# A scan-and-two-layers kernel: block coupling of the inverse done by matmuls in the chain, decays loaded once, other layouts, larger weight pieces and a new cost table for the order

## Chip, cores and metric

One core of a Trainium2 chip runs the whole program. The metric is device time in microseconds (us): the median of several executions. A profile is one execution more, recorded by the hardware profiler.

## What is computed

A recurrent attention over 768 steps for 4 x 8 heads of width 40 (float32), then two layer pairs with float64 weights on the 3072 tokens that it gives.

```python
for t in range(S):                      # S = 768, state (4, 8, 40, 40)
    y[:, :, t] = einsum('bhd,bhde->bhe', rt, state)
    Sa = einsum('bhde,bhe->bhd', state, at)
    state = state * wt[:, :, None, :] - einsum('bhd,bhe->bhde', Sa, bt) + einsum('bhd,bhe->bhde', vt, kt)
x = y as (3072, 320)
x = max(x @ w1, x @ w2, x @ w3) @ w_out             # d_ff 768
out = ((x @ w_a) * (x @ w_b)) @ w_out2              # d_ff 1536
```

## The kernel before

**The scan in chunks.** The 768 steps are cut into 24 chunks of 32, in 12 pairs. Within a chunk the recurrence is solved in closed form: products of decays (two scans on VectorE, DVE), matmuls of keys with the decayed a and b, and the inverse T of a unit triangular 32 x 32 matrix per head. `prep(p)` prepares pair p without the state, `chain(c)` carries the state through chunk c, `gather(p)` sends the pair's output through DRAM (XD) into the layout that the layers take (xf).

**Preparation.** `prep` loads the decays twice, forwards as wf into Pp and backwards as wr into Rp (line 376), the keys KT and a, b (ZL). Per chunk it scans Pp (line 396), takes the reciprocal of its end, scans Rp (line 400), multiplies keys (404) and ZL (414, POOL or DVE), runs matmuls (429 or 447), masks the result into ZL (435 or 454) and stores the 32 x 32 blocks to DRAM as BD (461). They come back one matrix to a partition as BU (467). `solve(p)` inverts on DVE and POOL: the two 16 x 16 diagonal blocks of each matrix by seven growing steps and two products (TW, TX), each a multiplication (501 on POOL, 502 on DVE) and a reduction (503). Then three more products give TC, the off-diagonal block times an inverse diagonal block; ACT lays out TU for them (535). T goes out as TD (473) and back as TT (477); TC goes out as ED (482) and back into NB (485), whose diagonal blocks are the identity.

**Chain.** In `chain(c)`: Z (620), copy Zs on ScalarE (ACT, 626); half (634) multiplies TT with Zs; copy Zy (638); umm (647) multiplies NB with Zy; copies XX, XU (657, 658); then the new state (held 672, smm 667, copies to ST and ZR) and, beside it, the output: transpose XT (703, 706), G (715), mask into YL (719), Y (733), scaling into XY (737). The values vt load into XT at 565.

**Layers.** `weights_a` cuts the float64 weights of the first layer pair into two float32r halves, in 24 pieces: a load (773), four conversions on DVE (763 to 766), copies (780), and for the first three of six blocks matmuls with the identity (790 to 793), for the others a subtraction and an addition (797, 798). `moe_a(p)` runs the first layer pair on the 256 tokens of pair p (841, 866 to 870) as soon as all its weights and xf are there, and stores X2D. `stage_b` cuts nine of the twelve blocks of the second layer pair's weights in 18 pieces into DRAM (WD, 933 to 941), `weights_b` loads them once the scan is done, `live_b` cuts the other three directly, and `moe_b(n)` runs the second layer pair on 512 tokens (995, 1003 to 1005), six times.

**What sets the order.** Nothing above is the order of issue. Every operation goes to a planner (`Plan`) with an engine, an estimated duration, what it reads and writes, PSUM banks and a priority (smaller first). `run` places one operation after another by these estimates; the result is one fixed order for each engine, and each engine executes it in order. DMAs go out on SyncE's queue (SP) in order, too: a DMA that waits holds up those behind it. `keep` inserts filler matmuls (line 277) where TensorE (PE) would be idle by plan. Eight PSUM banks are shared, with limits by kind (`LIMITS`).

Priorities: chain 0.001c, prep -0.5 + 0.6p, `weights_a` 2.0, `moe_a` 2 + p, `stage_b` 3.0, each less 0.04 times the remaining path.

## Time and profile before

| | us |
|---|---|
| median of 3 runs | 1065.24 (1064.34 to 1067.66) |
| the profiled execution | 1075.56 |
| its span, first to last instruction | 1073.8 |
| PE busy in the span | 1024.6 (95%) |
| DVE busy | 642.5 (60%) |
| ACT busy | 501.1 (47%) |
| POOL busy | 248.9 (23%) |

PE counts as busy while any matmul is in flight, so short waits hide under the end of the matmul before, and fillers count as work. A wait is put down to the event that came last. Start times are from the start of the span.

### The profile page before, as it was taken

Reading aid. Unit: us, or ns where it says so; the run is one execution under the profiler, and the core shown is the slowest. Engines: PE = TensorE matmul, PEld = TensorE weight load, DVE = VectorE, ACT = ScalarE, POOL = GpSimd, SP = SyncE. Lnnn points to the kernel's source line nnn. Section 1 sums busy time; section 2 is a strip of 40 time slices with the busy share of each in tenths; the row PEclk is TensorE's granted clock in tenths of the full one; section 3 lists DMA queues with packets and bytes.
Section 4 is the critical chain, followed back from the end, with each engine's and each line's share of the span. In section 5 each row is a group of like instructions: output and inputs, shape, how many; then the busy total and the mean of one; then the engine's idle time right before and its main releaser. Section 6 shows DMA issues by size and latency. Waiting matters only on the chain.

```text
span 1073.8 us, 34324 instructions
## 1 busy us (share of the span) xinstructions
PE 1024.6 (95%) x14888; PEld 920.8 (86%) x14888; DVE 642.5 (60%) x1046; ACT 501.1 (47%) x1157; POOL 248.9 (23%) x201
## 2 busy tenths in 40 slices
PE   8999888999899889989999999999999999999997
PEld 7877787988898888888899999888888888888886
DVE  7977688796789686979798333474232232332222
ACT  5337657476757566646567422243222232322221
POOL 3423366342336242343433100011000000000000
PEclk9989889899999999999999999999999999999999
DMA  8936966757776866666565448532001000000000
GB/s 271 207 75 147 195 149 140 166 133 187 162 187 143 198 159 146 169 165 169 152 167 136 115 125 246 144 97 74 1 11 45 1 26 1 7 19 1 25 1 28
DMA packets 173437, 123.10 MB, mean 115 GB/s; under 512 B 122464, under 2 KB 147168, under 8 KB 172320
## 3 DMA queue, kind: packets, MB, share of 16 engines
q1 hardware_dynamic: 170688, 116.41, 43.7%
q10 hardware_dynamic: 2592, 4.42, 1.2%
q8 instruction: 119, 1.95, 0.8%
q14 instruction: 38, 0.31, 0.1%
HBM read 93.07 MB, written 27.72 MB: 112 GB/s over the span
## 4 chain that ended last, share of the span: by engine, by line
PE 68%; DVE 11%; DMA 9%; issue 5%; ACT 3%; SPq 3%; POOL 1%; ACTq 0%; POOLq 0%; DVEq 0%
PE bank L995 25%; PE bank L841 11%; PE bank L1003 4%; PE bank L1005 4%; PE bank L1004 4%; PE bank L277 3%; DMA BU<-BD 2%; PE bank L733 2%; PE bank L715 2%; PE bank L647 1%; DMA WD<-wraw 1%; PE bank L866 1%; DVE TP L502 1%; DVE wraw L764 1%; PE bank L620 1%
## 5 line engine op out<-in xcount | busy, mean ns | idle before, releaser
L1013 DVE TENSOR_TENSOR bas<-bank,bas 128x512 f32<-128x512 f32 x72 | 49.7, 691 | 193.0 <-PE bank L995 186.5
L995 PE MATMUL bank<-bxhi,bw 128*128 128x512 f32 x576 | 156.3, 393 | 0.0
L995 PEld LDWEIGHTS bank<-bxhi,bw 128*128 128x128 f32 x576 | 106.0, 188 | 20.6
L1012 ACT ACTIVATE bas<-bank 128x512 f32<-128x512 f32 x72 | 43.0, 598 | 142.8 <-PE bank L995 142.8
L1015 ACT ACTIVATE bgh<-bas 128x512 fp32r<-128x512 f32 x72 | 45.5, 632 | 132.1 <-DVE bas L1013 132.1
L841 PE MATMUL bank<-xhi,whi 128*128 128x256 f32 x432 | 95.4, 303 | 0.0
L995 PE MATMUL bank<-bxlo,bw 128*128 128x512 f32 x288 | 89.7, 393 | 0.0
L841 PE MATMUL bank<-xhi,wlo 128*128 128x256 f32 x432 | 87.6, 284 | 2.1 <-issue 2.1
L841 PE MATMUL bank<-xlo,whi 128*128 128x256 f32 x432 | 87.9, 285 | 1.1 <-DVE xlo L830 1.1
L1003 PE MATMUL bank<-bo,bgh 128*128 128x320 f32 x288 | 88.9, 309 | 0.0
L1005 PE MATMUL bank<-bo,bgl 128*128 128x320 f32 x288 | 88.9, 309 | 0.0
L1004 PE MATMUL bank<-bo,bgh 128*128 128x320 f32 x288 | 88.8, 308 | 0.0
L856 DVE TENSOR_TENSOR hm<-bank,hm 128x512 f32<-128x512 f32 x72 | 49.5, 688 | 50.7 <-PE bank L841 46.7
L1016 DVE TENSOR_TENSOR bgl<-bas,bgh 128x512 fp32r<-128x512 f32 x72 | 50.4, 701 | 42.9 <-ACT bgh L1015 42.6
L414 POOL TENSOR_TENSOR ZL<-ZL,Pp 64x512 f32<-64x512 f32 x39 | 56.4, 1446 | 64.5 <-DVE Pp L396 51.2
L841 PEld LDWEIGHTS bank<-xlo,whi 128*128 128x128 f32 x432 | 67.9, 193 | 3.7 <-issue 2.2
L277 PE MATMUL bank<-con 128*128 128x128 f32 x482 | 67.6, 296 | 2.9 <-DMA con<-in_con_dram 2.9
L841 PEld LDWEIGHTS bank<-xhi,whi 128*128 128x128 f32 x432 | 66.7, 192 | 3.2
L277 PEld LDWEIGHTS bank<-con 128*128 128x128 f32 x482 | 62.7, 208 | 5.9 <-ACT bank L345 2.9
L841 PEld LDWEIGHTS bank<-xhi,wlo 128*128 128x128 f32 x432 | 67.4, 192 | 0.0
L995 PEld LDWEIGHTS bank<-bxlo,bw 128*128 128x128 f32 x288 | 54.1, 188 | 12.3
L841 PE MATMUL bank<-xl,wt 128*128 128x256 f32 x216 | 61.6, 285 | 0.4 <-DVE xl L834 0.4
(182 smaller groups left out, 2447.5 us busy)
## 6 DMA issues: line engine op xcount, KB each, us to landing
wraw<-in_wpb_dram SPq DMA_DIRECT2D x18, 480.0 KB
KT<-in_kb_dram SPq DMA_DIRECT2D x20, 384.0 KB
Pp<-in_wf_dram SPq DMA_DIRECT2D x10, 528.0 KB
Rp<-in_wr_dram SPq DMA_DIRECT2D x10, 528.0 KB
wraw<-in_wpa_dram SPq DMA_DIRECT2D x12, 384.0 KB
bw<-WD SPq DMA_DIRECT2D x9, 512.0 KB
WD<-wraw ACTq DMA_DIRECT2D x18, 240.0 KB
WD<-wca SPq DMA_DIRECT2D x18, 240.0 KB
```

Source lines behind the costliest of these rows:

```text
L277: P.keep = lambda b: T.matmul(bank[b][:, 0:128], ident, ident, start=True, stop=True)
L414: op("POOL", po(512), lambda w_, cc=cc, g=g, r0=r0: G.tensor_tensor(Z_[r0:r0 + 64, cc, g], Z_[r0:r0 + 64, cc, g], P_[r0:r0 + 64, cc, :, 0: ...
L841: T.matmul(ps, w, x, start=(i == 0), stop=(i == 7))
L856: op("DVE", dv(512, True), lambda w_, pn=pn: V.tensor_tensor(f(hm), bank[w_[pn]], f(hm), ALU.max), r=[pn], w=["hm"], fin=[pn], pri=ep)
L995: T.matmul(ps, w, x, start=(k == 0), stop=(k == 7))
L1003: T.matmul(o, gh[:, c], oh, start=ff == 0, stop=False)
L1004: T.matmul(o, gh[:, c], ol, start=False, stop=False)
L1005: T.matmul(o, gl[:, c], oh, start=False, stop=ff == 11)
L1012: op("ACT", ac(512), lambda w_, j=j, pa=pa: A.activation(tb["as", j], bank[w_[pa]], AF.Copy), r=[pa], w=[("bas", j)], fin=[pa], pri=ep)
L1013: op("DVE", dv(512, True), lambda w_, j=j, pb=pb: V.tensor_tensor(tb["as", j], bank[w_[pb]], tb["as", j], ALU.mult), r=[pb], w=[("bas", j) ...
L1015: op("ACT", ac(512), lambda w_, j=j, k=k: A.activation(tb["gh", k], tb["as", j], AF.Copy), r=[("bas", j)], w=[("gh", k)], pri=ep)
L1016: op("DVE", dv(512), lambda w_, j=j, k=k: V.tensor_tensor(tb["gl", k], tb["as", j], tb["gh", k], ALU.subtract), r=[("bas", j), ("gh", k)], ...
```

## The change

**Coupling.** For the first KS = 6 pairs `solve` returns after T: no TC, TU, ED. The off-diagonal block goes from BD straight into NB, whose diagonal blocks are zero. The chain runs half (T Zs), then lift, which adds NB times -T Zs to the bank of Z, a second copy into Zs, then last (T Zs) for the result. The bank of Z is freed after the second copy. From pair 6 on it is as before (with TU stored transposed).

**Decays.** One load Wp, in two halves of 48 partitions (64 in pair 0), feeds both scans; the second reads and writes backwards, into Rr. wr is gone.

**Values.** vt is stored with the head running fastest, so that each row of XT is one run of 2 KB; the copy of line 706 writes, and the weights of line 715 read, at a step of 16 elements.

**Pieces.** `weights_a` takes 12 pieces (768 and 512 columns) in place of 24, `stage_b` 9 pieces of 960 columns in place of 18. The buffers are larger.

**Order.** The planner gets new estimates: DMAs pass one after another at a fixed rate (`line`), POOL and DVE operations of two SBUF inputs exclude each other (`port`, `Both`), operations on PE are planned with a margin after what they wait for (`PMD`, `PME`), and a change of tile form on PE costs. Priorities: `weights_a` 0.3, `stage_b` 8.0, prep -0.5 + 0.45p.

```diff
+KS = 6
 NSPL = 2
 DMIN = 0.4
 NPB = 3
 NH = 2
-WP = 2.0
+WP = 0.3
...
-LAT = {"PE": 0.2, "ACT": 0.15, "DVE": 0.14, "POOL": 0.08}
+LAT = {"PE": 0.25, "ACT": 0.1, "DVE": 0.1, "POOL": 0.12}
+XRATE = 270e3
+XWAY = 1.8
+XISS = 0.46
+XQ = 1.0
+SLOPE = 0.45
+PMD = 0.7
+PME = 0.2
+PRE0 = -0.5
+EPA = 0.6
+GPR = 0.2
+SBP = 8.0
+MAP = 2.0
+MODE = 0.1
...
+                    if o["xfer"]:
+                        s = max(s, line - XQ)
+                    if eng == "POOL" or isinstance(o["ways"][eng][0], Both):
+                        s = max(s, port)
...
+            if eng == "POOL" or isinstance(o["ways"][eng][0], Both):
+                port = e
+            if o["xfer"]:
+                line = max(line, s + 1.0) + o["xfer"]
+                end = line + o["lat"]
...
+                mg = (PMD if o["xfer"] else PME) if "PE" in q else 0.0
+                est[j] = max(est[j], e if len(q) == 1 and eng in q and eng != "DVE" and o["lat"] is None else end + mg)
...
-        return 0.15 + n * 0.00105 if ps else 0.12 + n * 0.0014
+        return 0.15 + n * 0.00105 if ps else Both(0.13 + n * 0.00108)
 
     def ac(n):
-        return 0.17 + n * 0.0009
+        return 0.17 + n * 0.00086
 
     def po(n):
-        return 0.4 + n * 0.0023
+        return 0.2 + n * 0.0021
 
     def dma(fn, nbytes, r=(), w=(), pri=0.0, pre=1.2):
-        return op("SP", max(DMIN, nbytes / 300e3), fn, r=r, w=w, pri=pri, lat=1.4 + nbytes / 250e3, pre=pre)
+        return op("SP", XISS, fn, r=r, w=w, pri=pri, lat=XWAY, pre=pre, xfer=nbytes / XRATE)
...
+    Wp = ap_.tile([128, 2, NU * 33 + 1], F32, name="Wp")
+    Rr = ap_.tile([128, 2, NU * 33 + 1], F32, name="Rr")
+    Rp = [Rr[:, i, 1:NU * 33 + 1].rearrange("p (u s) -> p u s", s=33)[:, :, 1:33] for i in range(2)]
...
-            for t_, n, w in ((P_, "wf", [(k, b, c, g) for c in cs for k in ("P", "Pc") for g in range(2)]), (Rp, "wr", [(k, c, g) for c in cs for k in ("R", "Rc") for g in range(2)])):
-                dma(lambda w_, t_=t_, n=n, c0=c0, c1=c1: SP.dma_start(t_[:, c0:c1].rearrange("p c u s -> p c (u s)"), ia[n][p].rearrange("p (c f) -> p c f", c=2)[:, c0:c1]), 270e3 * (c1 - c0), w=w, pri=pr)
+            for g in range(2):
+                nr, src = (64, ia["wf0"][g]) if not p else (48, ia["wf"][p, g])
+                dma(lambda w_, g=g, nr=nr, src=src, c0=c0, c1=c1: SP.dma_start(Wp[GP[g]:GP[g] + nr, c0:c1], src[:, c0:c1]),
+                    nr * 2116 * (c1 - c0), w=[("W_", c, g) for c in range(c0, c1)], pri=pr)
...
-            op("DVE", 1.4, lambda w_, cc=cc: V.tensor_tensor_scan(
-                P_[:, cc].rearrange("p u s -> p (u s)"), P_[:, cc].rearrange("p u s -> p (u s)"),
+            op("DVE", Both(1.26), lambda w_, cc=cc: V.tensor_tensor_scan(
+                P_[:, cc].rearrange("p u s -> p (u s)"), Wp[:, cc, 0:NU * 33],
                 d1.rearrange("p u s -> p (u s)"), 0.0, ALU.mult, ALU.add), r=kp + ["d1"], w=pc, pri=pr)
-            op("DVE", 0.25, lambda w_, cc=cc: V.reciprocal(d1[:, :, 0:1], P_[:, cc, :, 32:33]), r=pc, w=["d1"], pri=pr)
-            op("DVE", 1.4, lambda w_, cc=cc: V.tensor_tensor_scan(
-                Rp[:, cc].rearrange("p u s -> p (u s)"), Rp[:, cc].rearrange("p u s -> p (u s)"),
+            op("DVE", 0.25, lambda w_, cc=cc: V.reciprocal(d1[:, :, 0:1], P_[:, cc, ::-1, 32:33]), r=pc, w=["d1"], pri=pr)
+            op("DVE", Both(1.26), lambda w_, cc=cc: V.tensor_tensor_scan(
+                Rr[:, cc, NU * 33:0:-1], Wp[:, cc, NU * 33:0:-1],
                 d1.rearrange("p u s -> p (u s)"), 0.0, ALU.mult, ALU.add),
-               r=[("R", cc, 0), ("R", cc, 1), "d1"], w=rc, pri=pr)
+               r=kp + ["d1"], w=rc, pri=pr)
...
+        nb = NB[p % 2]
+        if p in (KS, KS + 1):
+            unit(p % 2, pr)
+        if p < KS:
+            for j in range(4):
+                dma(lambda w_, j=j: SP.dma_start(
+                    nb[32 * j:32 * j + 16].rearrange("p c h t -> p (c h) t")[:, :, 16:32],
+                    BD[b].rearrange("(ch pqx) s t -> pqx s ch t", pqx=4)[j][0:16, :, 16:32]),
+                    16e3, r=bk, w=[("NB", p % 2, j)], pri=pr)
...
+        if p < KS:
+            return
...
-        prod(TC, 0, 16, BU, 16, 32, TU, 0, 16, 8, 8, 8, k, ["TC"])
-        prod(TC, 8, 16, BU, 16, 32, TU, 8, 16, 8, 8, 16, k, ["TC"])
+        prod(TC, 0, 16, BU, 16, 32, TU, 0, 1, 8, 8, 8, k, ["TC"], 16)
+        prod(TC, 8, 16, BU, 16, 32, TU, 128, 1, 8, 8, 16, k, ["TC"], 16)
...
-        dma(lambda w_: SP.dma_start(XT[0:80, :, 0, :], ia["vt"][c].rearrange("p (u t) -> p u t", t=32)),
-            328e3, w=[("XTv", 0), ("XTv", 1)], pri=pr, pre=4.0 if c else 1.2)
+        dma(lambda w_: SP.dma_start(XT[0:80, 0:C * NU], ia["vt"][c]),
+            260e3, w=[("XTv", 0), ("XTv", 1)], pri=pr, pre=4.0 if c else 1.2)
...
-                                     Z_[:, cc, g, bb * 4 + j, :], ZR[z][:, g, bb * 2 + pq, 1 - x, :], start=True, stop=True)
-
-        op("PE", 0.95, zmm, act=0.23,
+                                     Z_[:, cc, g, bb * 4 + j, :], ZR[z][:, g, bb * 2 + pq, 1 - x, :], start=p >= KS or (bb == 0 and g == 0), stop=p >= KS, skip_group_check=p < KS)
...
+        def lift(w_):
+            for k in range(8):
+                for j in range(4):
+                    T.matmul(bank[w_[pz]][32 * j:32 * j + 32, k * 40:k * 40 + 40],
+                             NB[p % 2][32 * j:32 * j + 32, cc, k, :], Zy[32 * j:32 * j + 32, k, :], start=False, stop=True, skip_group_check=True)
+
+        def last(w_):
+            for bb in range(B):
+                for g in range(2):
+                    for j in range(4):
+                        k, n = g * 4 + bb, bb * 2 + g
+                        T.matmul(bank[w_[pu]][32 * j:32 * j + 32, n * 40:n * 40 + 40],
+                                 T_[32 * j:32 * j + 32, cc, k, :], Zs[32 * j:32 * j + 32, k, :], start=True, stop=True)
+
+        if p < KS:
+            op("PE", 0.72, lift, md="32", r=["Zy"] + [("NB", p % 2, j) for j in range(4)], w=[pz], act=0.045, pri=pr)
+            op("ACT", ac(320), lambda w_: A.activation(
+                Zs.rearrange("p k d -> p (k d)"), bank[w_[pz]][:, 0:320], AF.Copy, scale=-1.0), r=[pz], w=["Zs"], fin=[pz], pri=pr)
+            op("PE", 0.72, last, md="32", r=["Zs"] + [("TT", b, j) for j in range(4)], w=[pu], ps=[pu], act=0.045, pri=pr)
+        else:
+            op("PE", 0.72, umm, md="32", r=["Zy"] + [("NB", p % 2, j) for j in range(4)], w=[pu], ps=[pu], act=0.045, pri=pr)
...
-                    T.matmul(ps[64 * x:64 * x + 64, u * 64:u * 64 + 64], XT[0:80, 2 * u + x].rearrange("p k s -> p (k s)"), RB[0:80, :, 2 * u + x], start=True, stop=True)
-
-        op("PE", 1.26, gmm, r=[("XTu", 0), ("XTu", 1), ("XTv", 0), ("XTv", 1), ("RB", 0), ("RB", 1)], w=[pg], ps=[pg], act=0.45, pri=0.2 + pr)
+                    T.matmul(ps[64 * x:64 * x + 64, u * 64:u * 64 + 64], XT[0:80, 2 * u + x::NU], RB[0:80, :, 2 * u + x], start=True, stop=True)
...
+            for q in range(1):
+                pr = SBP
+                cs = slice(0, 960)
+                dma(lambda w_, ff=ff, cs=cs: SP.dma_start(r, ia["wpb"][ff][:, cs].bitcast(U32).rearrange("p (m k) -> p m k", k=2)), 983e3, w=wk + ["sr", "sw"], pri=pr)
+                convert(lambda: r, lambda: a, 960, "sr", "sa", pr, w=ck)
```

## Rows read from the trace of the kernel before

**Rows 1.** Busy time by stage: stage, us; each engine's busy us; granted clock, DMA.
```profile
0.00:150.00 150.00, 137.02 (x2604) 116.83 (x2605) 118.95 (x195) 83.89 (x219) 63.05 (x57) 0.94 0.71 172
150.00:200.00 50.00, 44.23 (x937) 39.65 (x937) 38.75 (x68) 30.94 (x81) 24.67 (x20) 0.83 0.63 152
25.00:250.00 225.00, 207.58 (x4369) 180.50 (x4368) 185.56 (x304) 133.13 (x347) 100.25 (x82) 0.92 0.65 151
200.00:594.00 394.00, 369.51 (x8225) 342.06 (x8225) 318.18 (x525) 249.69 (x612) 149.90 (x113) 0.99 0.67 164
```

**Rows 2.** The same for line 277's fillers alone: PE, PEld, clock, DMA.
```profile
0.00:150.00 150.00, 55.79 (x392) 51.86 (x392) 0.94 0.71 172
```

**Rows 3.** PE's first layer matmul, and ACT's copies of weights with first and last start.
```profile
148.86 0.48 PE L841 MATMUL bank<-xhi,whi 128*128 128x256 f32 x2
...
L780 ACT ACTIVATE wt<-wraw x12: 357/368/391, 22.6 to 194.8; 64x192 fp32r<-64x192 f32 x12
```

**Rows 4.** End of the chain of waits through the scan: start us, us, what.
```profile
628.14 1.35 PE bank L733 x64
...
653.40 9.60 PE bank L841 x80
```

**Rows 5.** PE in order of time, half and umm of chunks 0, 1, 10, 11.
```profile
64.17 1.29 PE L634 MATMUL bank<-Zs,TT 32*32 32x40 f32 x64
74.16 0.79 PE L647 MATMUL bank<-Zy,NB 32*32 32x40 f32 x64
87.78 0.79 PE L634 MATMUL bank<-Zs,TT 32*32 32x40 f32 x64
91.85 1.06 PE L647 MATMUL bank<-Zy,NB 32*32 32x40 f32 x64
298.94 0.79 PE L634 MATMUL bank<-Zs,TT 32*32 32x40 f32 x64
311.73 0.79 PE L647 MATMUL bank<-Zy,NB 32*32 32x40 f32 x64
322.91 0.97 PE L634 MATMUL bank<-Zs,TT 32*32 32x40 f32 x64
327.77 0.79 PE L647 MATMUL bank<-Zy,NB 32*32 32x40 f32 x64
```

**Rows 6.** Chunk 6: Z in the chain of waits, then half on PE.
```profile
190.69 1.23 PE bank L620 x64
...
214.92 0.42 PE L634 MATMUL bank<-Zs,TT 32*32 32x40 f32 x4
```

**Rows 7.** DVE groups of 0 to 250 us: busy us, mean ns | idle before.
```profile
L502 DVE TENSOR_TENSOR TP<-BU,TU 128x512 f32<-128x512 f32 x7 | 8.3, 1185 | 4.7 <-ACT TU L535 4.7
L503 DVE TENSOR_REDUCE TC<-TP 128x32 f32<-128x512 f32 x10 | 6.7, 677 | 0.0
L503 DVE TENSOR_REDUCE TC<-TP 128x64 f32<-128x512 f32 x5 | 3.4, 673 | 0.0
```

**Rows 8.** DVE in order of time, one conversion of 384 and one of 192 columns.
```profile
68.04 0.56 DVE L764 SCALAR_TENSOR_TENSOR wraw<-wraw,wca 128x384 uint32<-128x384 uint32 x1
86.05 0.36 DVE L764 SCALAR_TENSOR_TENSOR wraw<-wraw,wca 128x192 uint32<-128x192 uint32 x1
```

**Rows 9.** Mask of pair 5's blocks on DVE, then SP's queue, in order of time.
```profile
248.56 1.73 DVE L435 TENSOR_TENSOR ZL<-bank,con 64x256 f32<-64x256 f32 x4
...
255.75 2.44 SPq L485 DMA_DIRECT2D NB<-ED  x2
...
259.93 0.97 SPq L461 DMA_DIRECT2D BD<-ZL  x2
```

**Rows 10.** PE's line 715 in the chain of waits; DVE with and without steps.
```profile
622.08 1.08 PE bank L715 x32
...
70.80 1.04 DVE L502 TENSOR_TENSOR TP<-TW,TXp 128x512 f32<-128x512 f32 x1
250.32 0.69 DVE L859 TENSOR_TENSOR hlo<-hm,hhi 128x512 fp32r<-128x512 f32 x1
```

More of the change, by code (lines that the diff above doesn't have):

```diff
@@ L109, in run @@
         done, last, top = 0, 0, 0.0
+        line, port, mode = 0.0, 0.0, None
         busy = {}
@@ L154, in run @@
                         f = s + o["ways"][eng][0] + o["ways"][eng][2]
-                        if any(max(free_t.get(e, 0.0), est[i]) + w[0] + w[2] < f for e, w in o["ways"].items() if e != eng):
+                        if any(max(free_t.get(e, 0.0), est[i], port if e == "POOL" or isinstance(w[0], Both) else 0.0) + w[0] + w[2] < f for e, w in o["ways"].items() if e != eng):
                             continue
@@ L207, in run @@
                     dur *= 2
+                if o["md"] != mode:
+                    dur += MODE if o["md"] else 0.0
+                elif mode:
+                    dur -= MODE
+                mode = o["md"]
                 spend(s, s + dur, o["act"])
@@ L230, in run @@
                 q = self.ops[j]["ways"]
-                est[j] = max(est[j], e if len(q) == 1 and eng in q and eng != "DVE" and o["lat"] is None else end)
+                mg = (PMD if o["xfer"] else PME) if "PE" in q else 0.0
+                est[j] = max(est[j], e if len(q) == 1 and eng in q and eng != "DVE" and o["lat"] is None else end + mg)
                 if not left[j]:
@@ L350, in setup @@
         for i in range(2):
-            op("ACT", ac(512), lambda w_, i=i: A.activation(
-                NB[i].rearrange("p c h t -> p (c h) t"), TC.rearrange("p i j -> p (i j)")[:, 0:32].unsqueeze(1).to_broadcast([128, 16, 32]), AF.Copy), r=["TC"], w=[("NB", i, j) for j in range(4)], pri=-3)
+            zero(NB[i], [("NB", i, j) for j in range(4)], "POOL", pri=-3)
         dma(lambda w_: SP.dma_start(TXp, ia["eye"]), 270e3, w=["TX"], pri=-0.55)
@@ L385, in prep @@
         for cc in range(2):
-            kp = [("P", b, cc, g) for g in range(2)]
+            kp = [("W_", cc, g) for g in range(2)]
             pc = [("Pc", b, cc, g) for g in range(2)]
@@ L409, in prep @@
+            op("POOL", 2.25, kmul(G), r=rc + [("K", kb_, cc, 0), ("K", kb_, cc, 1)], w=kc, pri=pr, alt=[("DVE", dv(1024), kmul(V))])
+            for src, k, n in ((Rp[cc], rc, 1), (P_[:, cc, :, 1:33], pc, 0)):
                 op("ACT", 0.61, lambda w_, cc=cc, src=src, n=n: A.activation(
-                    Rp[:, cc, :, 0:32], src, AF.Square, accum_out=gd[:, 4 * p + 2 * cc + n:4 * p + 2 * cc + n + 1]),
+                    Rp[cc], src, AF.Square, accum_out=gd[:, 4 * p + 2 * cc + n:4 * p + 2 * cc + n + 1]),
@@ L480, in prep @@
                 130e3, r=[("TD", b, h) for h in range(2)], w=[("TT", b, j)], pri=pr)
-        for h in range(2):
+        for h in range(2 if p >= KS else 0):
             dma(lambda w_, h=h: SP.dma_start(ED[b][:, 8 * h:8 * h + 8, :], TC[64 * h:64 * h + 64]), 33e3, r=["TC"], w=[("ED", b, h)], pri=pr)
-        nb = NB[p % 2]
-        for j in range(4):
+        for j in range(4 if p >= KS else 0):
             dma(lambda w_, j=j: SP.dma_start(
@@ L488, in prep, with unit @@
                 16e3, r=[("ED", b, h) for h in range(2)], w=[("NB", p % 2, j)], pri=pr)
+    def unit(i, pr):
+        op("ACT", ac(512), lambda w_: A.activation(
+            NB[i].rearrange("p c h t -> p (c h) t"), con[:, 192:224].unsqueeze(1).to_broadcast([128, 16, 32]), AF.Copy), r=["con"], w=[("NB", i, j) for j in range(4)], pri=pr)
     def solve(p):
-        pr = -0.5 + 0.6 * p
+        pr = PRE0 + SLOPE * p
         cnt = [0]
@@ L635, in half @@
                              T_[32 * j:32 * j + 32, cc, k, :], Zs[32 * j:32 * j + 32, k, :], start=True, stop=True)
-        op("PE", 0.9, half, r=["Zs"] + [("TT", b, j) for j in range(4)], w=[ph], ps=[ph], act=0.045, pri=pr)
-        op("ACT", ac(320), lambda w_: A.activation(Zy.rearrange("p k d -> p (k d)"), bank[w_[ph]][:, 0:320], AF.Copy), r=[ph], w=["Zy"], fin=[ph], pri=pr)
+        op("PE", 0.72, half, md="32", r=["Zs"] + [("TT", b, j) for j in range(4)], w=[ph], ps=[ph], act=0.045, pri=pr)
+        op("ACT", ac(320), lambda w_: A.activation(Zy.rearrange("p k d -> p (k d)"), bank[w_[ph]][:, 0:320], AF.Copy, scale=1.0 if p >= KS else -1.0), r=[ph], w=["Zy"], fin=[ph], pri=pr)
         pu = ("a", "u", c)
@@ L910, in open_w @@
             tb["gl", i] = w.tile([128, 512], F32R, name=f"bgl{i}")
+        for i in range(2):
+            tb["lr", i] = w.tile([128, 1024], F32, name=f"blr{i}")
+            tb["lc", i] = w.tile([128, 512], F32, name=f"blc{i}")
     def open_x():
@@ L1208, in layout @@
     o["aa"] = pair(em(a)).reshape(NP, 2, D, 2, -1)
-    for n in ("wf", "wr"):
-        z = np.ones((NP, 2, 64, 2, NU, 33), f)
-        z[..., 0] = 0
-        z[:, :, 0:D] = o[n].reshape(NP, 2, D, 2, NU, 33)
-        o[n] = z.reshape(NP, 128, -1)
+    z = np.ones((NP, 2, 64, 2, NU * 33 + 1), f)
+    z[..., ::33] = 0
+    z[:, :, 0:D] = pair(wf).reshape(NP, 2, D, 2, NU * 33 + 1)
+    o["wf"], o["wf0"] = np.ascontiguousarray(z[:, :, 0:48]), np.ascontiguousarray(z[0])
     for n, m in (("kb", 2),):
```

171 lines of the change are left out of this document (79 added, 92 removed).

## The prediction

> **What bounds the kernel now.** I read the page first, then the table of stages, then TensorE's lines in order of time, then DVE's and the DMA queue's around one pair. The page has TensorE (PE) busy nearly throughout; the reader is to see that this is not a full PE. By stage, the span of 1073.8 us is 673 us of scan with the first layer pair, and 400 us of the second layer pair, whose matmuls the change leaves alone; I carry these 400 us over. In the first 150 us, 55.8 of the 137.0 busy us are the filler matmuls of line 277 [rows 1, 2]. From 150 to 200 us the granted clock averages 0.83, that is some of the time at 1.2 instead of 2.4 GHz, which loses 0.17 x 50 = 8.5 us, and PE idles 5.8 us [rows 1]; the first layer of pair 0 begins at 148.9 and is held up there, since the last of its weights are cut at 194.8 [rows 3]. From 200 to 594 us PE idles 24.5 us [rows 1]. So most of the loss lies in the first 200 us, and the end is PE's backlog behind the chain: the last chunk's output matmuls start at 628.1 and the backlog runs to 673 without a gap [rows 4].
>
> What feeds PE is the chain of 24 chunks, and that is fed by the preparation of each pair (loads, scans, inverse, round trips over DRAM). From 25 to 250 us DVE is busy 185.6 of 225 us, 82% [rows 1]: this engine sets the pace of the early preparations. A preparation shows twice in the chain: as a wait for the inverse T ahead of the half matmuls (line 634), and as a wait for the coupling block NB ahead of line 647.
>
> **The change part by part.** The sum is made against the profiled execution (span 1073.8, its time 1075.56 us). That stands 10.3 us, 1%, above the median of the three runs, 1065.24; I take the difference in us off the median.
>
> Coupling on PE. In the first six pairs NB no longer needs three products and three reductions on DVE or POOL and the round trip TC, ED, NB; it comes straight from BD. For that each of 12 chunks runs half, lift, last in place of half, umm: one more group of 64 matmuls and one more ACT copy, both inside the dependent chain. Call the time from the start of one group to the start of the next dependent one a step. Half to umm took 9.99, 4.08, 15.18, 4.29, 8.96, 12.79 us in the six first chunks, 55.3 in all, and 4.07, 7.14, 3.91, 1.86, 3.12, 4.86 us in the six second ones, median 4.0; the first and the last of each six are in [rows 5]. First chunks wait for NB, second ones show the bare step. Its bounds are therefore 1.9 and 7.1 us; I take 3.5, near the median. First chunks: 6 x 2 x 3.5 = 42 against 55.3, a gain of 13. Second chunks: 6 x 3.5 = 21 more. Of these I let four of six hide, because the next pair's half waits for T anyway (24 us in chunk 6 [rows 6]): 7 remain. Net -6, with bounds -33 (12 x 1.9 against 55.3, all second ones hidden) and +73 (12 x 7.1 against 55.3, and 6 x 7.1 more). PSUM bank z is now held from Z through the wait for T, out of eight; what that costs is inside the upper bound. PE's own work grows by 12 groups of at most 0.79 us [rows 5], 9 us. Half falls into the first 200 us, where fillers cover it: +4, bounds 0 and +9. Where that cover is gone, it is the 9.
>
> DVE's relief. In the first 250 us the removed products and reductions cost DVE 8.3 + 6.7 + 3.4 = 18.4 us [rows 7]. Of the weight pieces, four conversions for each of 24 pieces become four for each of 12. Two conversions of 192 columns take 2 x 0.36 us against 0.56 for one of 384 [rows 8], 0.16 more; four times that is 0.64 us for a piece saved, times 12 = 7.7 us. Together 26 us, and at DVE's 82% share 21 us of the early preparations: -21, bounds 0 (something else comes last) and -26.
>
> Decays once. The second decay load is gone, and the first keeps 64 or 48 rows of 128. By the shapes the first two pairs load 0.95 MB instead of 2.16, 1.2 MB less, which at the 172 GB/s of the first 150 us [rows 1] is 7 us of transfers; only part of it stands in front of the first inverse: -3, bounds -7 and 0. Both scans now read one buffer (a reload must wait for both scans of the pair before, and what SP has queued behind that load waits too). This costs nothing while a load has most of a pair's time, some 45 us; if that cover goes, it is one load's latency in a pair. Reversed reading covers as many elements; I take the scan's time as unchanged.
>
> SP's queue. ED and NB stand in order with all else. At chunk 8 SP is with NB from 255.75 on, and the BD store of the next pair, ready at 250.3, goes out at 259.9 [rows 9]. With ED gone from six preparations and half as many weight loads such delays are rarer; but the NB loads stay, and loads of 983 KB, twice the old size, now stand in front of small ones. The bytes are the same, hits half as often and twice as long: I take -2, bounds -10 (one such delay) and +10.
>
> Values in long rows. 1280 short runs a chunk become 80 long ones. No long wait of PE for them is in the trace, so 0. The price is elsewhere: the weights of line 715 are now read at a step of 64 bytes. The trace has no strided weight load; these 32 matmuls take 1.08 us at unit step. The nearest strided row is DVE's product of 512 with one operand at a large step, 1.04 us against 0.69 for a unit-step subtraction [rows 10]: a factor 1.5, which here is 24 x 0.54 = 13 us. Bounds 0 and 13; I take 0, since weight loads overlap matmuls. The Trainium skill, "SBUF — State Buffer", section "SBUF: two separate sides", speaks against this edit: SBUF is read in lines of 16 bytes, and accesses that each go to a new line pay a penalty, so that fp32 strides about four elements for free; this one strides sixteen. By that rule the 13 us would belong in the sum, by TensorE's own row nothing.
>
> Order with room. Weight pieces move from priority 2.0 to 0.3, ahead of the preparations of pairs 2 and up; the cutting of the second layer pair's weights moves behind. If the first pieces are cut by about 150 us instead of 195, pair 0's first layer (192 matmuls at the 0.12 us of [rows 4], 23 us) falls into time that holds fillers and idle now. That lets PE's backlog at the end shrink as much as the chain does; without it the chain's gain only lengthens the backlog. I cost it at 0, and T is what comes last again.
>
> Sum: -6 + 4 - 21 - 3 - 2 = -28, so 1065 - 28 = 1037 us.
>
> **The rivals.** (1) More. PE also gets back what the sum leaves lying: half of the 24.5 us idle from 200 to 594 (12), the 8.5 us of clock, the 7 us of second chunks. That is -28 - 27 = -55, 1010 us. For it: 55.8 us of fillers are room enough. Against: T is still waited for. (2) The strided weights cost their 13 us on a full PE: 1050 us; the skill's rule would make it so. (3) No relief. T is set by DMA round trips, not by DVE, so the 21 us fall away, and half the strided price (6) eats the rest: 1064 us. For it: the six first chunks lose 55 us to a round trip. (4) A long step. If ACT and PE place other work between half, lift and last, the step is 5 us, not 3.5, and if T comes early enough that nothing hides, the chain changes by 12 x 5 + 6 x 5 - 55.3 = +35; with the other terms (-22) that is +13, 1078 us. It decides from a step of 77.3/18 = 4.3 us on. For it: one step took 7.14 us, and the median is 4.0. Against: waits for T like that of [rows 6].
>
> **How the numbers follow.** Forecast 0.49 (its own range, about half the way to the bounds of its two largest terms, 1022 to 1054), more 0.20, strided 0.07, no relief 0.08, long step 0.16. Faster by over 0.3%, which is about what a measurement of this kernel can tell from no change: 0.49 + 0.20 + 0.07 = 0.76; within it 0.08; slower 0.16. The range reaches from somewhat below the second case to short of the last, 1004 to 1073, and leaves out a tail of the fast case and most of the slow one.
>
> **What would show it.** Right: the last chunk's output matmuls start near 600 instead of 628; half to lift and lift to last are 3 to 4 us each; 18 reductions into TC instead of 36; the last weights are cut before 160 and pair 0's first layer is done by about 180; fillers in the first 150 us are well below 56; the 32 matmuls of line 715 still take 1.08 us. Wrong: steps above 4.3 us, T as late as now in pairs 2 to 5, or more idle time of PE between 200 us and the end of the chain, which an order made from misjudged durations would show.

## The result and the profile after

| | before | after |
|---|---|---|
| median of 17 runs, us | 1068.24 (1064.34 to 1074.50) | 1075.79 (1073.44 to 1079.86) |
| ratio, 95% interval | | 1.0073 (1.0053 to 1.0092) |
| span of the profiled execution, us | 1073.8 | 1072.2 |
| PE busy, us | 1024.6 | 1039.1 |
| DVE, POOL busy, us | 642.5, 248.9 | 596.8, 133.1 |

The change makes the kernel slower by 0.7%, some 8 us. The forecast was 1037 us, 28 us of gain. The two profiled executions differ by less than the medians, and the other way: that of before (1075.56 us, granted clock 0.980) took longer than any of its 17 runs, and that of after (1073.94 us, clock 0.990) is the second shortest of its 17, whose clocks average 0.985. So the traces tell where the time sits, and the ratios tell how much it is.

Busy time by stage, as in [rows 1]: stage, us, then PE, PEld, DVE, ACT, POOL, granted clock, DMA share, GB/s.

```profile
0.00:150.00 150.00, 142.34 (x3093) 121.22 (x3097) 107.61 (x177) 84.49 (x219) 27.24 (x28) 0.99 0.67 166
150.00:200.00 50.00, 45.85 (x1010) 42.38 (x1001) 38.34 (x54) 29.68 (x72) 14.41 (x14) 0.93 0.46 122
25.00:250.00 225.00, 215.32 (x4969) 187.39 (x4967) 165.01 (x272) 136.70 (x346) 46.29 (x40) 0.98 0.58 144
200.00:594.00 394.00, 378.97 (x8735) 356.03 (x8734) 288.72 (x492) 265.95 (x622) 89.71 (x79) 0.99 0.59 151
```

DVE has its relief: 165.0 of 225 us from 25 to 250 where [rows 1] have 185.6, and POOL falls from 100 to 46. The granted clock of that stretch is 0.98 and was 0.92. PE idles 15.0 us from 200 to 594, down from 24.5. Everything that was to feed PE better does so.

The fillers of the first 150 us (line 313 now, as in [rows 2]), and the start of the first layer with the last cut of a weight (as in [rows 3]):

```profile
0.00:150.00 150.00, 51.56 (x390) 48.34 (x390) 0.99 0.67 166
```

```profile
157.16 0.51 PE L909 MATMUL bank<-xhi,whi 128*128 128x256 f32 x2
```

```profile
L854 ACT ACTIVATE wt<-wraw x12: 359/370/394, 51.4 to 199.2; 64x192 fp32r<-64x192 f32 x12
```

The weights are not cut earlier: 199.2 against 194.8, the first layer starts at 157.2 against 148.9, and the fillers are nearly as many.

The last of the first layer's matmuls, before and after: count, ns, first and last start.

```profile
L841 PE MATMUL bank<-xl,wt x216: 277/283/415, 149.9 to 672.3; 128*128 128x256 f32 x108
L909 PE MATMUL bank<-xl,wt x216: 279/283/415, 158.1 to 670.4; 128*128 128x256 f32 x108
```

The chain of waits at its end, as in [rows 4]: start us, us, what.

```profile
603.91 2.04 PE bank L786 x32
...
609.00 1.35 PE bank L804 x64
...
651.45 9.60 PE bank L909 x80
```

The last chunk's output starts at 609.0, 19 us earlier than the 628.1 of [rows 4]. But the longest run of first-layer matmuls stands at 651.5, where it stood at 653.4: the lead of the chain is gone 40 us later, and the first layer ends at 670.4 where it ended at 672.3. And the G group takes 2.04 us, where [rows 10] have 1.08.

PE around half (685), lift (704) and last (712) in chunks 0 and 10, as in [rows 5]:

```profile
55.27 0.79 PE L685 MATMUL bank<-Zs,TT 32*32 32x40 f32 x64
58.23 0.79 PE L704 MATMUL bank<-Zy,NB 32*32 32x40 f32 x64
60.27 0.79 PE L712 MATMUL bank<-Zs,TT 32*32 32x40 f32 x64
...
289.46 0.79 PE L685 MATMUL bank<-Zs,TT 32*32 32x40 f32 x64
292.01 0.54 PE L704 MATMUL bank<-Zy,NB 32*32 32x40 f32 x34
...
295.51 0.79 PE L712 MATMUL bank<-Zs,TT 32*32 32x40 f32 x64
```

The steps are short: 2.96 and 2.04 us, 2.55 and 3.50 us; over all twelve chunks the 24 steps average 3.23 us.

PE's busy time in the fillers and in G, before and after, then in lift: busy us, mean ns, idle before it.

```profile
L277 PE MATMUL bank<-con 128*128 128x128 f32 x482 | 67.6, 296 | 2.9 <-DMA con<-in_con_dram 2.9
...
L715 PE MATMUL bank<-RB,XT 80*64 80x64 f32 x768 | 29.6, 232 | 3.6 <-issue 2.3 <-ACT XT L706 0.6 <-DMA RB<-in_rb_dram 0.6
...
L313 PE MATMUL bank<-con 128*128 128x128 f32 x488 | 66.0, 291 | 7.9 <-DMA con<-in_con_dram 3.0 <-DVE ZL L491 2.7 <-issue 1.2
...
L786 PE MATMUL bank<-RB,XT 80*64 80x64 f32 x768 | 50.1, 282 | 1.4 <-issue 0.9 <-ACT XT L777 0.5
...
L704 PE MATMUL bank<-Zy,NB 32*32 32x40 f32 x768 | 10.3, 202 | 2.4 <-issue 2.4
```

### The profile page after: what moved, and what is told of

Same layout as the page of the kernel before. It is cut to its first block, busy times and chain, and to the rows that moved or that the text cites. A ratio compares the mean times of both kernels' runs of the same rounds, so it can differ in the third digit from the quotient of the medians.

```text
span 1072.2 us, 35552 instructions
## 1 busy us (share of the span) xinstructions
PE 1039.1 (97%) x15662; PEld 940.9 (88%) x15662; DVE 596.8 (56%) x984; ACT 509.5 (48%) x1139; POOL 133.1 (12%) x121
## 4 chain that ended last, share of the span: by engine, by line
PE 92%; DMA 3%; DVE 2%; issue 2%; ACT 1%; SPq 0%; POOL 0%; DVEq 0%; POOLq 0%
PE bank L1063 25%; PE bank L909 18%; PE bank L313 6%; PE bank L786 4%; PE bank L1073 4%; PE bank L1071 4%; PE bank L1072 4%; PE bank L804 3%; PE bank L934 2%; PE bank L484 2%; PE bank L738 2%; PE bank L628 2%; PE bank L466 2%; PE bank L685 2%; PE bank L645 2%
## 5 line engine op out<-in xcount | busy, mean ns | idle before, releaser
L1080 ACT ACTIVATE bas<-bank 128x512 f32<-128x512 f32 x72 | 43.1, 598 | 134.1 <-PE bank L1063 131.6
L909 PE MATMUL bank<-xt,wt 128*128 128x256 f32 x216 | 61.6, 285 | 0.0
```

The lines of the kernel that those rows point to most:

```text
L909: T.matmul(ps, w, x, start=(i == 0), stop=(i == 7))
L1080: op("ACT", ac(512), lambda w_, j=j, pa=pa: A.activation(tb["as", j], bank[w_[pa]], AF.Copy), r=[pa], w=[("bas", j)], fin=[pa], pri=ep)
```

## The experiments

Ratios are to the kernel before on the same chip, with a 95% interval. Three names from the expectations: theory A is "the strided weights are the loss", rival B is "the new order is the loss", and theory C, formed after the first four runs, is "the coupling costs more than it gives". The kernels of the change without the strides (e1_near) and without strides and coupling (e5_near_ks0) are the bases of most of the others.

| run | what it is | ratio |
|---|---|---|
| e1_near | after, XT as before | 1.0032 (1.0002 to 1.0063) |
| e2_far | before, only the strided values | 1.0059 (1.0022 to 1.0096) |
| e3_quad | after, step of 16 bytes | 1.0116 (1.0062 to 1.0171) |
| e5_near_ks0 | e1_near without the coupling | 0.9905 (0.9870 to 0.9940) |
| e4_ks0 | after without the coupling | 1.0031 (0.9963 to 1.0099) |
| e6_near_ks12 | e1_near, coupling in twelve pairs | 1.0174 (1.0113 to 1.0234) |
| e7_order | after in the old order | 1.0499 (1.0444 to 1.0553) |
| e8_couple | before with the coupling alone | 1.0168 (1.0112 to 1.0224) |
| r1_relief | e5_near_ks0, products left out in six pairs | 0.9875 (0.9832 to 0.9919) |
| r2_cost | e1_near, products computed as well | 1.0303 (1.0264 to 1.0341) |
| r4_spare | e5_near_ks0, 12 spare groups | 1.0071 (1.0041 to 1.0101) |
| e10_near_order_ks0 | e5_near_ks0 in the old order | 1.0269 (1.0216 to 1.0322) |
| e11_pieces_undone | e5_near_ks0 with small pieces | 1.0059 (1.0028 to 1.0089) |
| e12_decays | before with the decays alone | 1.0151 (1.0099 to 1.0203) |
| c1_ks6_bl, c2_ks6_sl | e1_near in two other orders | 0.9984 (0.9951 to 1.0017), 0.9850 (0.9822 to 0.9877) |
| c3_ks0_bl, c4_ks0_sl | e5_near_ks0 in two other orders | 1.0001 (0.9976 to 1.0026), 0.9943 (0.9911 to 0.9976) |

**The strides.** Three kernels in which the instructions of every engine stand in the same order as in the kernel they are compared with; only XT's layout differs.

e1_near:

```diff
-    XT = ap_.tile([128, 2 * C * NU], F32, name="XT")
+    XT = ap_.tile([128, NU, 2, 32], F32, name="XT")
...
-    T.matmul(..., XT[0:80, 2 * u + x::NU], RB[...], ...)
+    T.matmul(..., XT[0:80, 2 * u + x].rearrange("p k s -> p (k s)"), RB[...], ...)
```

> The changed kernel with the tile XT as it was before (value rows of 32 beside state rows of 32, so a weight is 64 numbers in a row) and every other part of the change kept; the order on the five engines stays as it is. Theory A, the strided weights are the loss: the 24 G groups fall from 2.01 to about 1.08 us, TensorE gets 24 x 0.93 = 22 us less, and since it is 97% busy the time falls by nearly all of that, from 1075.8 to about 1054 (1050 to 1060), and ScalarE's copies into XT fall from 1.07 to 0.59 us. Rival B, the new order is the loss (weights still cut until 199 us, filler matmuls as many as before) and the strides lie in waits: under 6 us, so 1070 to 1076.

e2_far is the same diff turned round, on the kernel before.

> The kernel before with only the value part of the change: long value rows, weights with a step of 64 bytes, everything else old. Theory A: the G groups rise from 1.08 to 2.01 us; TensorE was less full before, and the chain of the blocks ended at 628 us, so between half of the 22 us and, with the chain prolonged by 24 x (0.93 + 0.48) = 34 us, all of it: 1079 to 1100, most likely 1088. Rival B: under 6 us, 1066 to 1074.

e3_quad:

```diff
-    XT = ap_.tile([128, 2 * C * NU], F32, name="XT")
+    XT = ap_.tile([128, NU // 4, 2, 32, 4], F32, name="XT")
...
-    T.matmul(..., XT[0:80, 2 * u + x::NU], RB[...], ...)
+    T.matmul(..., XT[0:80, (2 * u + x) // 4, :, :, (2 * u + x) % 4].rearrange("p k s -> p (k s)"), RB[...], ...)
```

> The changed kernel with XT in four blocks of four sub-blocks: value rows of 512 bytes in place of 2048 or 128, and weights with a step of 16 bytes (64 bytes in the change, 4 in the first of these runs). It asks from which step on TensorE's weights cost more. If a step within 16 bytes is read at full rate, the G groups take 1.08 us and the time is that of the first run of these, about 1054. If every step other than one costs the same, they take 2.01 us and the time is 1076. A value between (1.3 to 1.6 us) would show a cost that grows with the step, 1060 to 1068.

The tile XT in the traces of after, e1_near and e3_quad in turn: engine, operation, count: shortest, median and longest ns, first and last start.

```profile
L786 PEld LDWEIGHTS bank<-RB,XT x768: 185/209/228, 65.7 to 605.6; 80*64 80x64 f32 x192
L786 PE MATMUL bank<-RB,XT x768: 273/280/338, 65.7 to 605.7; 80*64 80x64 f32 x192
...
L777 ACT ACTIVATE XT<-bank x24: 1037/1068/1120, 64.6 to 602.0; 80x512 f32<-80x512 f32 x24
```

```profile
L786 PEld LDWEIGHTS bank<-RB,XT x768: 132/138/227, 65.0 to 599.2; 80*64 80x64 f32 x192
L786 PE MATMUL bank<-RB,XT x768: 216/222/315, 65.0 to 599.3; 80*64 80x64 f32 x192
...
L777 ACT ACTIVATE XT<-bank x24: 574/593/596, 64.2 to 596.6; 80x512 f32<-80x512 f32 x24
```

```profile
L786 PEld LDWEIGHTS bank<-RB,XT x768: 192/216/218, 65.5 to 608.8; 80*64 80x64 f32 x192
L786 PE MATMUL bank<-RB,XT x768: 281/283/332, 65.5 to 608.9; 80*64 80x64 f32 x192
...
L777 ACT ACTIVATE XT<-bank x24: 1092/1114/1199, 64.3 to 605.3; 80x512 f32<-80x512 f32 x24
```

A strided weight load takes 209 ns and not 138, the matmul behind it 280 and not 222. The step of 16 bytes costs as much as the step of 64. ScalarE's copy into XT changes with the same edit, so the times below are the price of both. The G groups alone account for 24 x (2.04 - 1.08) = 23 us of PE. In time it is less: 1.0073 - 1.0032 = 0.4% from after to e1_near, 1.0116 - 1.0032 = 0.8% from e3_quad, 0.6% from before to e2_far, so 4 to 9 us, a fifth to two fifths of it; each of the three is clear of zero by its intervals, but not by much. Theory A expected 22 us and falls; rival B (under 6 us) is nearer. The rest lay in waits: PE's idle time and fillers are 99 us in after and 109 us in e1_near (table below).

**The coupling undone.**

```diff
-KS = 6
+KS = 0
```

> The first of these runs with the coupling undone too: in all twelve pairs VectorE and GpSimd couple the two halves, as in the kernel before; decays, pieces and order stay changed. Against the first run TensorE loses 12 lifts of 0.72 us, 8.6 us, and the 18 reductions of the coupled block come back to VectorE. If TensorE alone is the bound from the first layers on, the time falls by up to 8 us, to about 1046. If the chain's lead is worth what the forecast said, VectorE's 21 us come back: 1065 to 1075. My guess lies between, no more than 5 us either way.

> The changed kernel with the coupling alone undone (VectorE and GpSimd couple the halves in all twelve pairs; strided values, decays, pieces and order stay changed). Theory C, the coupling costs more than it gives: TensorE gets 12 lifts of 0.72 us, 8.6 us, and groups with little activity during which its clock falls (mean granted clock 0.990 without it and 0.983 with it), while VectorE's relief ends in waits that no longer set the end; the time then falls by 10 to 16 us against the changed kernel, to 0.993 to 0.998 of before. Theory A, the strides are the loss and the coupling is a gain: no fall, 1.007 to 1.02 of before.

With XT as before the kernel gets faster by 1.3%; with the strides the intervals overlap. e6_near_ks12 sets KS = 12:

> The changed kernel with XT as before and the coupling on TensorE in all twelve pairs in place of six. Theory C (a cost for each coupled pair): the six more pairs cost again what the first six did, 10 to 14 us over the run with six (1.003 of before), so 1.012 to 1.017. If only the first pairs' coupling hurts (where TensorE waits for the chain), the time stays within 5 us of that run. If VectorE's relief is a gain in the later pairs, it falls.

e8_couple brings only the diff's lines for the coupling (`unit`, `lift`, `last`, NB straight from BD, the early return in `solve`) into the kernel before:

> The kernel before with the coupling of the first six pairs on TensorE and nothing else changed. My forecast gave the coupling by itself about 20 us of gain (0.98 of before). Theory C: a loss, from 12 lifts of 0.72 us and a lower clock against what VectorE's 18 reductions each pair give back, 1.00 to 1.013 of before.

(The last expectation should read 18 reductions in all, three a pair.) Up to here all but e4_ks0 agreed with theory C in sign, e6_near_ks12 and e8_couple a little above its ranges: each coupled variant was 1.3 to 1.7% slower than its partner.

**The order undone.** e7_order takes the planner, its prices and its priorities from before:

```diff
-WP = 0.3
+WP = 2.0
...
-LAT = {"PE": 0.25, "ACT": 0.1, "DVE": 0.1, "POOL": 0.12}
+LAT = {"PE": 0.2, "ACT": 0.15, "DVE": 0.14, "POOL": 0.08}
...
-SLOPE = 0.45
+SLOPE = 0.6
...
-SBP = 8.0
+SBP = 3.0
```

> The changed kernel with the planner, its prices and its priorities as they were before (weights' priority, the slope over the pairs, latencies, no shared port, no common transfer line); coupling, decays, strided values and pieces stay. It asks what 'order with room' is worth. My forecast had 0 for it. Theory C says the order is a gain that the other parts eat: without it the time is 5 to 15 us longer than the changed kernel (1.012 to 1.022 of before). If the order is the loss (rival B), it is shorter: 0.995 to 1.003.

It is 4.2% slower than after, more than either theory had: with the rest of the change in place, the order is the largest single difference. No run gives the new order to the kernel before.

**Where the coupling's price lies.** r1_relief is e5_near_ks0 with the products left out:

```diff
-        if p < KS:
+        if p < 6:
             return
```

> VectorE's relief alone. XT as before, no coupling on TensorE, and the products that couple the halves on VectorE and GpSimd left out in the first six pairs (a part of the computation is left out: those pairs use a block of zeros in its place). Against the same kernel with the products (0.9905 of before) my forecast would give about 20 us, so 0.972. Theory C, VectorE and GpSimd no longer set the end and the chain of the blocks is paced by TensorE: within 4 us, 0.987 to 0.994.

r2_cost is e1_near without that return, so that both ways are computed:

> The coupling's cost alone. XT as before, the coupling on TensorE in the first six pairs as in the change, and the products on VectorE and GpSimd computed all the same, though nobody reads them. Theory C: as slow as the run with the coupling and without the products, 1.003 of before, at most 5 us longer, since the relief is worth little. By my forecast the relief is what pays: 20 us longer, 1.02.

r4_spare is e5_near_ks0 with one more group a chunk into a bank of its own:

```diff
+        if p < 6:
...
+            op("PE", 0.72, spare, md="32", r=["Zy"] + [("NB", p % 2, j) for j in range(4)], w=[pd], ps=[pd], fin=[pd], act=0.045, pri=pr + 0.2)
```

> XT as before, no coupling on TensorE, and in each of the first twelve chunks one spare group of 32 small matmuls like a lift, into a bank that nobody reads, beside the chain and not in it. It parts TensorE's time for the lifts from the longer chain. If their 12 x 0.72 us and their low activity are the cost, it is as slow as the coupled kernel: 9 to 14 us over 0.9905, so 0.999 to 1.003. If the cost is that the chain has one more turn from TensorE to ScalarE and back in each chunk, it stays within 4 us of 0.9905.

Three views of e5_near_ks0, then of r1_relief: busy time over the whole span (columns as above), the fillers, and DVE's reductions into TC.

```profile
0.00:1054.30 1054.30, 1023.36 (x15078) 926.31 (x15078) 620.20 (x1014) 505.41 (x1145) 152.54 (x127) 0.99 0.45 109
L313 PE MATMUL bank<-con 128*128 128x128 f32 x672 | 86.6, 284 | 4.3 <-DMA con<-in_con_dram 2.9 <-issue 0.7 <-DVE YL L790 0.7
L552 DVE TENSOR_REDUCE TC<-TP 128x32 f32<-128x512 f32 (+1 forms) x36 | 24.1, 676 | 1.5 <-POOL TP L550 1.2
```

```profile
0.00:1059.90 1059.90, 1027.81 (x15046) 930.85 (x15046) 594.91 (x990) 494.23 (x1127) 132.86 (x116) 0.99 0.44 109
L313 PE MATMUL bank<-con 128*128 128x128 f32 x640 | 85.3, 290 | 2.8 <-DMA con<-in_con_dram 2.8
L553 DVE TENSOR_REDUCE TC<-TP 128x32 f32<-128x512 f32 (+1 forms) x18 | 12.2, 679 | 1.2 <-POOL TP L551 1.2
```

DVE is relieved of 18 reductions and 25 us, and PE's waits stay: 30.9 idle and 86.6 of fillers with the products, 32.1 and 85.3 without. The ratio gains 0.3%, within the intervals. r4_spare has 10.4 us of spare groups (line 728 below) and no longer chain, its fillers stay, and it is 1.7% slower: in this one order the groups beside the chain cost their whole time and more. But r2_cost, 2.7% above e1_near, says that the same products do cost when the chain is coupled as well. By one path (relief first) the relief is worth 3 us and the coupling then costs 17; by the other the coupling costs 42 and the relief gives back 29. The filler line of r4_spare and its spare groups:

```profile
L313 PE MATMUL bank<-con 128*128 128x128 f32 x666 | 89.2, 290 | 6.4 <-DMA con<-in_con_dram 2.9 <-DVE ZL L491 1.8 <-ACT Zs L677 0.6
...
L728 PE MATMUL bank<-Zy,NB 32*32 32x40 f32 x768 | 10.4, 202 | 3.3 <-issue 3.3
```

Where r2_cost loses its time the traces show: from 200 to 350 us PE is busy 121.7 of 150 us at a granted clock of 0.89, and in e1_near 137.6 at 0.98 (r2_cost first, columns as above).

```profile
200.00:350.00 150.00, 121.72 (x2644) 109.76 (x2632) 120.02 (x199) 80.69 (x191) 19.48 (x16) 0.89 0.56 145
200.00:350.00 150.00, 137.59 (x3306) 127.09 (x3305) 112.14 (x188) 98.17 (x239) 28.41 (x26) 0.98 0.67 155
```

**Decays and pieces.** e10_near_order_ks0 puts e5_near_ks0 into the old order, as e7_order did with after:

> XT as before, no coupling on TensorE, and the planner with prices and priorities as before; what is left of the change is decays once and larger weight pieces. Against the same kernel with the new order (0.9905) it shows what the order is worth without the other two parts; with them it was 44 us. If the order is a gain by itself, 10 to 40 us over 0.9905, 1.00 to 1.03. If it was only that the old prices don't fit the coupling and the strides, within 5 us of 0.9905. My forecast had 3 us of gain for the decays, 0 for pieces and order: 0.997.

It is 3.6% slower than e5_near_ks0. In the profiled executions it has 135.3 us of fillers and idle time against 117.5, and the same number of other matmuls takes 965.5 us against 936.8, at a mean granted clock of 0.965 against 0.994.

e11_pieces_undone is e5_near_ks0 with before's `weights_a` and `stage_b`; e12_decays is the same in the old order.

```diff
-            pieces(w[:, 0:768], 768, lambda: wraw[0], lambda: wca[0], ...)
...
+            for kt in range(2):
+                for (c0, c1) in ((0, 384),):
+                    piece(m, w[:, kt * 384 + c0:kt * 384 + c1], c1 - c0, ...)
```

> XT as before, no coupling on TensorE, new order and decays kept, and the weights in pieces of 384 and 480 columns as before. Against the same kernel with the larger pieces (0.9905 of before): my forecast had 0 for the pieces. If the larger pieces are a gain (fewer, longer instructions on VectorE and fewer loads on the queue), 0.993 to 1.005. If they are the loss that the kernel with the old order showed (1.027 of before, with only decays and pieces left of the change), the time falls by up to 29 us, to 0.965 to 0.985.

> Of the change only the decays are left: XT, coupling, pieces, planner, prices and priorities are those of before. My forecast had 3 us of gain for the decays, 0.997. If the loss of the kernel with decays and pieces in the old order (1.027) comes from the pieces, this is 0.99 to 1.00; if it comes from the decays, 1.02 to 1.03.

In the new order the small pieces cost 1.5%, and the trace has a place. PE's waits in e11_pieces_undone from 600 to 760 us: what PE waited for, us in total, times, longest.

```profile
PE bank L1069 <- DMA bw<-WD: 10.4, 1, 10.4
PE bank L1069 <- ACT bw L854: 2.3, 1, 2.3
```

The second layer pair waits for its weights; in e5_near_ks0 PE waits for nothing in this stretch. Nor does it behind the first layer in the kernels of the old order: from the last first-layer matmul to the end e7_order and e10_near_order_ks0 take 401.8 and 401.7 us, as before does (401.5), and e11_pieces_undone 425.0. So this wait belongs to the new order with small pieces and is no part of what the old order costs. Old order against new is 0.9% with small pieces (1.0151 and 1.0059) and 3.6% with large ones (1.0269 and 0.9905).

**The control.** Each change of content makes the planner place everything anew. Four kernels give it another weight for the work ahead or another slope; the work stays as it is, and only fillers and the planner's choice between DVE and POOL move with the order:

```diff
-BL = 0.04
+BL = 0.042
```

```diff
-SLOPE = 0.45
+SLOPE = 0.46
```

> A control. XT as before and the coupling on TensorE in six pairs, with nothing else changed but the planner's weight for the work still ahead (0.042 in place of 0.04): the same instructions in another order. If the coupling's price of 14 us is its own, this stays near 1.003 of before (0.998 to 1.010). If such differences are chances of the order, it may fall anywhere, 0.985 to 1.02.

> A second control with the coupling: the priority's slope over the pairs 0.46 in place of 0.45. As for the first: near 1.003 if the coupling's price is its own.

> A control without the coupling: XT as before, VectorE and GpSimd couple in all pairs, and the planner's weight for the work ahead 0.042 in place of 0.04. Near 0.9905 of before (0.985 to 0.997) if the coupling's price is its own; anywhere in 0.985 to 1.02 if the order decides.

> A second control without the coupling: the slope over the pairs 0.46 in place of 0.45. Near 0.9905 if the coupling's price is its own.

With the coupling the three orders give 1.0032, 0.9984 and 0.9850, mean 0.9955; without it 0.9905, 1.0001 and 0.9943, mean 0.9950. The scatter of the order alone is 1.8% with the coupling, 1.0% without, and the means differ by less than 0.1%; with three orders of each, one standard error of that difference is 0.6%, 6 to 7 us. So theory C is not borne out either, in the size that I had given it: the 14 us between e1_near and e5_near_ks0 can be two draws, that is two accidents of the order. e6_near_ks12, e8_couple, r1_relief, r4_spare, e11_pieces_undone and e12_decays rest on one draw each, and differences below about 1.5% among them are not settled. Above that scatter stand e7_order and e10_near_order_ks0 (against after and e5_near_ks0), and r2_cost, each in one order too. The scatter was measured with the new planner only: no run gives the kernel before, or any other of the old order, a second order. All four of the old order that were placed anew (e7_order, e8_couple, e10_near_order_ks0, e12_decays) are slower than before, so before may itself be a good draw of its order; that is untested.

What PE's time consists of, in the profiled executions (busy and idle over the span; fillers by their line; work is busy less fillers; then the last start of a matmul of the output's line 733 or 804, and of a first-layer matmul, L1). The work column moves with the granted clock too: e5_near_ks0 and c3_ks0_bl have the same matmuls, at 0.994 and 0.988.

| kernel | span | PE work | fillers | PE idle | fillers + idle | DVE busy | last output matmul | last L1 |
|---|---|---|---|---|---|---|---|---|
| before | 1073.8 | 957.0 | 67.6 | 49.2 | 116.8 | 642.5 | 629.3 | 672.3 |
| after | 1072.2 | 973.1 | 66.0 | 33.1 | 99.1 | 596.8 | 610.1 | 670.4 |
| e1_near | 1065.5 | 956.4 | 66.1 | 43.0 | 109.1 | 595.2 | 603.7 | 663.9 |
| c1_ks6_bl | 1066.5 | 953.7 | 72.1 | 40.8 | 112.9 | 605.3 | 591.0 | 664.8 |
| c2_ks6_sl | 1055.6 | 952.8 | 63.3 | 39.5 | 102.8 | 600.3 | 597.3 | 653.7 |
| e5_near_ks0 | 1054.3 | 936.8 | 86.6 | 30.9 | 117.5 | 620.2 | 598.6 | 652.1 |
| c3_ks0_bl | 1063.5 | 946.4 | 86.7 | 30.4 | 117.1 | 625.8 | 611.9 | 661.6 |
| c4_ks0_sl | 1050.5 | 935.9 | 89.1 | 25.5 | 114.6 | 616.5 | 583.1 | 649.1 |

The span is the last L1 plus 401 to 402 us in every row. With the coupling PE has 15 us more work (954 against 940 in the mean), of which the lifts are some 10, and 8 us less of fillers and idle time; the fillers' part falls by 20 and the idle part rises by 12. In these single executions the coupled three are 6 us longer in the mean; over all runs the ratios say no difference. The fillers of c2_ks6_sl and c4_ks0_sl, the fastest of either kind:

```profile
L313 PE MATMUL bank<-con 128*128 128x128 f32 x478 | 63.3, 287 | 4.1 <-DMA con<-in_con_dram 3.0 <-DVE XY L808 1.1
```

```profile
L313 PE MATMUL bank<-con 128*128 128x128 f32 x700 | 89.1, 282 | 5.0 <-DMA con<-in_con_dram 2.9 <-ACT Zs L677 1.9 <-ACT XU L729 0.2
```

So the lifts may stand where the planner would otherwise put fillers; that is argued from these sums, and r4_spare, whose fillers did not fall, speaks against it. c2_ks6_sl, with the coupling and without the strides, and e5_near_ks0, without either, are faster than both kernels of this case (0.9850 and 0.9905 of before).

## Why the prediction was wrong

It had the sign wrong, and the time lies above its range. By its steps:

**What bounds the kernel: half right.** PE was named as never full, and the chain as what feeds it, with DVE as its pace. The chain did end 19 us earlier, near the 600 that I had asked for. The step that failed is the next one: that the lead reaches the end. The sum carries what DVE and the chain gain, -21 and -6, to the end of the kernel one for one. But the first layer's last matmul starts at 670.4 instead of 672.3, and from there to the end both kernels take the same 401.5 to 401.8 us. In the profiled executions PE's waits (fillers and idle time) fell by 17.7 us (116.8 to 99.1), and its work rose by 16.1 (957.0 to 973.1). The sum had +4 for PE's added work; the lines say +20.5 for G (29.6 to 50.1 us) and +10.3 for the lifts, less 14.7 that the other lines lost. Some 10.7 us is what the higher clock of that execution is worth (0.990 against 0.980 of 1073 us, an estimate), so at equal clocks the work would have risen by more than the waits fell. "Without it the chain's gain only lengthens the backlog", the prediction said under the order; that is what happened.

**Coupling, -6 + 4: the steps right, the total not.** The 24 steps average 3.23 us, the forecast 3.5; the two steps of the six first chunks take 32.3 us against 55.3, better than the 42 taken. Rival 4 (a mean step above 4.3 us) did not come, though three of the 24 steps were longer (5.04, 4.36 and 5.75 us). But with and without the coupling three orders average the same, so half, lift and last together with the products' relief are worth 0, give or take those 6 to 7 us, where I had -17: -6, +4 and, of the -21, the products' 18.4 of 26 us, some -15.

**DVE's relief, -21: the largest wrong term.** DVE's share from 25 to 250 us fell about as foreseen (82% to 73%). In r1_relief, which has the products' relief (15 of the 21) and nothing else, PE's waits stay at 117 us and the time moves by 0.3%, 3 us; against the mean of the three orders without the coupling it is 0.75%, 8 us. I had read the pace of the preparations from a busy share. A share of 82% with no row showing PE waiting for DVE was no price. In r2_cost the products do cost, 2.7%; why they weigh there and not in r1_relief is open. And the chain's earlier end isn't the relief's: its last output matmul starts at 583 to 612 us without the coupling, at 591 to 604 with it, and in e8_couple, coupled in the old order, at 636.6. It came mostly with the new order: the kernels of the old one have it at 620 to 639, those of the new one at 583 to 617, but for e4_ks0 (625.4) and r2_cost (629.6).

**Values in long rows, 0: wrong.** The one row that I let overrule the strided one ("weight loads overlap matmuls") did not hold here: with loads 71 ns longer the matmuls take 58 ns more, and a group of 32 takes 2.04 us instead of 1.08. The nearest row's factor 1.5 was too small, G grew by 1.9 [rows 10]. In time it is 4 to 9 us, inside my bounds of 0 and 13. The rule of the Trainium skill ("SBUF — State Buffer", section "SBUF: two separate sides") spoke against this edit and was right on the sign. Of what it says the runs agree with one part: accesses that each go to a new line of 16 bytes pay, and a step of 64 bytes (209 ns) costs no more than one of 16 (216 ns), against 138 ns without. That fp32 may step four elements for free they do not bear out: four elements are the 16 bytes of e3_quad. Whether the line decides, or any step other than one costs the same, they can't tell: no run has a step of 8 or 12 bytes.

**Order with room, 0: wrong the other way.** Its stated way didn't come: weights cut until 199.2, pair 0's first layer from 157.2. Yet the old order costs 4.2% on after and 3.6% on e5_near_ks0. In the profiled executions that is more fillers and idle time (134.1 us in e7_order against 99.1, 135.3 in e10_near_order_ks0 against 117.5) and more time for the same work, at a lower mean granted clock (0.974 against 0.990, 0.965 against 0.994). Which of the planner's changes does it was not tried.

**Decays, -3.** One kernel has them alone, in the old order, 1.5% slower; one draw of the order, within the scatter, so open. SP's queue, -2, was not tried by itself.

**Together.** Strides 4 to 9 us, coupling with relief 0 (give or take 6 to 7), the rest about -5 us (0.995, the mean of three orders): that makes -1 to +4 us, and the measured ratio is +8. The remaining 4 to 9 us lie inside the 1.8% by which the same work scatters with its order, and cannot be laid on a part. Rival 3 ("no relief") had the mechanism, with a time (1064) some 12 us too low.

## What to carry over

On an engine that is busy 95%, first list the work that a change adds to that engine, group by group, and count the gain of a relieved engine only where a row shows the full one waiting for it. The list is not yet the time: here 23 us of G cost 4 to 9. Operand layout is part of that work: in all three pairs contiguous weights with short DMA rows were the faster choice. Where a planner places everything anew, time two or three orders of the same work before a difference of 1% is laid on the edit.

## What the hardware showed

Weights of 64 fp32 columns at a step load in 209 to 216 ns and not 138, whether the step is 16 or 64 bytes; ScalarE's copy of 80 x 512 into the same stepped tile takes 1068 to 1114 ns and not 593. The prediction had the first hidden under the matmuls and no term for the second. Within the runs of one kernel the time follows the mean granted clock: over 29 runs of before on one chip it lies between 0.974 and 0.988 of 2.4 GHz, and 0.01 of it goes with 9 us.
